# Value products of the last three head pairs: from whole float32 to split 16-bit form

## The chip, the cores and the metric

The kernel runs on one core of a Trainium2 chip. The metric is the device time of one execution in microseconds (us), the median of several runs. TensorE does the matrix products, VectorE and ScalarE work on SBUF and PSUM, GpSimd works on SBUF and issues its own DMAs, and SyncE issues most of the other DMAs.

## The reference

Block-causal attention over 8 batches, 8 heads, 576 positions and 64 columns a head, and behind it a mixture of experts with one expert per token:

```python
scores = scale * np.matmul(q, k.transpose(0, 1, 3, 2))
mask = block_i >= block_j            # blocks of 64 positions
scores = np.where(mask, scores, -1e9)
attn = np.exp(scores - np.max(scores, axis=-1, keepdims=True))
attn = attn / (np.sum(attn, axis=-1, keepdims=True) + 1e-09)
x = np.matmul(attn, v)               # to (4608, 512)
...
e_idx = np.argmax(x @ w_gate, axis=1)
...
h = np.maximum(x[mask] @ w1[e], 0.0) # for each expert e and its tokens
out[mask] = gate_w[mask, None] * eom[mask, e, None] * (h @ w2[e])
```

All inputs and the output are float32.

## The kernel before

Attention works on 32 pairs of heads (pair p is two heads of one batch; four pairs make a batch). The 576 keys of a head are four blocks of 128 (block c is 0 to 3) and an odd block of 64. The work is written out by hand as rounds g = 0 to 135: in each round fixed steps of several pairs are emitted, and each engine executes its instructions strictly in the order of emission. For pair p:

- `prob_tile(3)` in round 4p+4, `prob_tile(0)` and `prob_tile(1)` in 4p+5 and `prob_tile(2)` in 4p+6 compute the scores on TensorE and their exponentials on ScalarE (line 254). Tile 3 holds the odd keys, tile 0 the blocks 1 and 3, tile 1 block 0, tile 2 block 2; the exponentials are float32 in `pcr`, `pc13`, `pc0` and `pc2`.
- `lows(i)` on GpSimd (line 263) makes the low part of a tile: the float32 value less the bfloat16 that is its upper half, stored as float16 (`lpcr` for the odd keys, `lpc` for the others). Tiles 0 and 1 take two instructions, one for each head; tiles 2 and 3 take one.
- `split_v` makes from the loaded values `vn` a float16 high part `vh` (ScalarE, line 155) and a float16 low part `vl` (GpSimd, line 156). It stands in round 4p+7, for the last four pairs in 4p+6.
- `values_odd` multiplies the odd keys' exponentials with the values, and `values(0)` and `values(1)` those of the four blocks for head 0 and head 1: ten products of a 128x128 block with 65 columns per head. They come in rounds 4p+10 and 4p+11, earlier or later for the last pairs: pair 29 in 126 and 127, pair 30 in 129 and 131, pair 31 in 132 and 133. `norm` on VectorE (lines 306 to 310) follows, and then the store and the transposition `turn_x` (line 323).

A block is multiplied in one of two forms. The split form (`splits`, lines 272 to 274) is three 16-bit products: high part with `vh`, high part with `vl`, low part with `vh`. The whole form (line 296) is one float32 product of the exponentials with `vn`; it needs neither `lows` nor `split_v` for that block. `self.whole` lists the blocks that take the whole form: none up to pair 27, block 0 for pair 28, all four for pairs 29, 30 and 31. The odd keys are always split.

Between these steps the rounds carry the start of the expert part. GpSimd scatters the sorted slots of each batch to a table (`tab_d`, line 622), clears the row buffers (line 1072, round 121), reads ids from the table (line 810, round 122) and gathers the first rows (line 821, three gathers at the end of round 124, behind `lows(3)` and ahead of the other `lows` of pair 30). From round 126 on each round casts one quarter of the first expert's weights on ScalarE (line 849) and subtracts on VectorE (line 851: the float32 weights less their high part, both in SBUF), `w1b` first and then `w2b`. SyncE loads the weights (line 885) and the values, and stores the rows. After round 133 come the first expert's products (line 973).

Of the kernel before, what the change touches and what calls it, by code (L numbers as in the profile page):

```python
# [26 lines left out]
def block_attention_top1_moe(  # L27
# [41 lines left out]
    NPR = B * NP  # L69
# [22 lines left out]
    class Pair:  # L92


        def __init__(self, p):
            self.p = p
            self.b, self.hp = divmod(p, NP)
            self.tr = {}
            self.whole = (0, 1, 2, 3) if p >= NPR - 3 else (0,) if p == NPR - 4 else ()

        def fetch(self, queue=None):
            h0 = 2 * self.hp
# [38 lines left out]
        def odd(self, c, ab, c0, c1):  # L141
            return self.tr[c][64 * ab:64 * ab + 64, 0, c0:c1]
# [8 lines left out]
                )  # L151

        def split_v(self):
            sl = slice(2 * len(self.whole), 10)
            nc.scalar.copy(self.vh[:, sl, 0:D], self.vn[:, sl, 0:D])  # L155
            nc.gpsimd.tensor_tensor(self.vl[:, sl], self.vn[:, sl, 0:D], self.vh[:, sl, 0:D], ALU.subtract)  # L156

# [95 lines left out]
                ap = ps[:, :, 0:320]  # L253
            last_exp[0] = nc.scalar.activation(self.pt[i], ap, AF.Exp, scale=SCALE)  # L254

        def lows(self, i):
            if i < 3 and ((1, 3), (0,), (2,))[i][0] in self.whole:
                return
            eng = nc.gpsimd
            n = 2 if i < 2 else 1  # L260
            for ab in range(n):
                sl = slice(ab, ab + 1) if n == 2 else slice(0, 2)
                eng.tensor_tensor(self.pl[i][:, sl], self.pt[i][:, sl], self.high(i)[:, sl], ALU.subtract)  # L263

# [67 lines left out]
    def turn_max(p):  # L332

        z = pairs[p]
        ps = banks()
        pm = ps[:, 0].bitcast(BF16)
        for t in range(NT):
            nc.tensor.transpose(pm[:, P * t:P * t + P], z.nmz[:, t, :], identb)
        z.qe = sb.tile([P, 640], BF16, name="qe")
        nc.scalar.copy(z.qe, pm[:, 0:640])  # L340

    def turn_rest(p, p9):

        ps = banks()
        flat = ps.rearrange("p a n -> p (a n)")
        x = pairs[p].turn_x(flat) if 0 <= p < NPR else iter(())
        y = pairs[p9] if p9 < NPR else None
        next(x, None)
        if y:
            y.turn_blocks(ps[:, 1:2, P:2 * P], 0)  # L350
        next(x, None)
        if y:
            y.halves(ps[:, 1:2, P:2 * P], 0)

    def third(p, between=None):

        ps = banks()
        x, y = (pairs[p] if p < NPR else None), (pairs[p - 1] if p else None)
        if x:
            x.odds([ps[:, ab] for ab in range(2)], 3, 320)  # L360
        if y:
            y.prob_tile(2, ps)
        if between:
            between()
        if x:
            x.max_tile(2)
            last_max[0] = nc.vector.tensor_reduce(x.nm3[:, 1], ps[:, :, 320:384], AX.X, ALU.max, negate=True)
            x.max_rest()
# [70 lines left out]
    def at(g, fn):  # L439
        events.setdefault(max(g, 0), []).append(fn)  # L440

    def opening():


        x, y = Pair(0), Pair(1)
        x.fetch(nc.scalar)
        y.fetch()

        def turned(z, late, ps=None):
            z.turn(owing, ps)  # L450
            one = banks()[:, 0:1, 0:P]
            z.turn_blocks(one, 0)
            z.halves(one, 0, late)

        main = ps_v.tile([P, 2, 512], F32, name="ps_v")
        for i in range(NWARM):
            nc.tensor.matmul(main[:, i % 2], zero16[:, 0:P], zero16, start=True, stop=True)
        turned(x, None, main)
        second.append(lambda: turned(y, owing))
        return x, y  # L460

    with tc.manual_schedule(engines={mybir.EngineType.PE}), tc.high_priority(offset=2000):
        pairs = dict(enumerate(opening()))
# [51 lines left out]
    def pay_later(kind=None):  # L515
        for g in list(later):
            if kind is None or want.get(g) in (None, kind):
                want[g] = next(g, later)
                if want[g] is later:
                    later.remove(g)  # L520
# [529 lines left out]
        at(4 * p - 14, lambda p=p: make(p))  # L1050
    for p in range(NPR):
        at(4 * p + 1, lambda p=p: pairs[p].fetch_v())
        at(4 * p + 6 + (p < NPR - 4), lambda p=p: pairs[p].split_v())
        at(min(4 * p + 13, 4 * NPR + 7), lambda p=p: pairs[p].store())
    at(6, constants)

# [34 lines left out]
    def round_of(g):  # L1091

        r = g % 4

        z = pairs[NPR - 1] if g >= 4 * NPR else None

        def do(back, name, *args):
            p = (g - back) // 4
            if 0 <= p < NPR - (name in LATE):
                getattr(pairs[p], name)(*args)  # L1100

        if r == 0:
            do(4, "prob_tile", 3)
            do(0, "max_tile", 0)
            if g != 4 * NPR:
                do(12, "norm")
            if g == 4 * NPR + 4:
                z.values_odd()
                z.values(0)
            do(4, "lows", 3)  # L1110
        elif r == 1:
            do(5, "prob_tile", 0)
            do(5, "prob_tile", 1)
            do(1, "max_tile", 1)
            do(5, "lows", 0)
            do(5, "lows", 1)
            if g == 4 * NPR + 1:
                pairs[NPR - 2].values_odd()
                pairs[NPR - 2].values(0)
            if g == 4 * NPR + 5:  # L1120
                z.values(1)
                z.norm()
                next(ahead)
                turn_rest(NPR - 2, NPR)
                next(ahead)
        elif r == 2:
            odd = (lambda: do(10, "values_odd")) if g != 4 * NPR + 2 else None
            if g // 4 <= NPR:
                third(g // 4, odd)
            elif odd:  # L1130
                odd()
            while second:
                second.pop(0)()
            while owing:
                owing.pop(0)()
            if g != 4 * NPR + 2:
                do(10, "values", 0)
            if g > 2:
                do(-6, "turn")
            pay_later("m")  # L1140
            pay_later("n")
            pay_later("v")
            do(6, "lows", 2)
        else:
            if g < 4 * NPR:
                turn_max(g // 4)
            if g == 3:
                pairs[2].turn()
            if g < 4 * NPR + 4:
                turn_rest(g // 4 - 3, g // 4 + 2)  # L1150
            else:
                turn_rest(NPR - 1, NPR)
            pay_later("x")
            do(11, "values", 1)
            if g == 4 * NPR - 1:
                pairs[NPR - 3].norm()
        for fn in events.get(g, ()):
            fn()
        pay_later("abwy"[r])
# [4 lines left out]
    with tc.manual_schedule(engines={AT.PE, AT.Activation, AT.DVE, AT.Pool}):  # L1164
        for g in range(NG):
            round_of(g)
            for i in range(FIRST.get(g, 0)):
                next(ahead)
        for what in "papaap":
            if what == "a":  # L1170
                next(ahead)
            else:
                pay_later()
        while later:
            next(ahead, None)
            pay_later()
# [116 lines left out]
```

## Time and profile before

| | before |
|---|---|
| runs | 753.75, 759.34, 760.31 us; median 759.34 |
| profiled execution | 754.9 us, its span 753.3 us |
| TensorE busy | 93% |
| VectorE busy | 68% |
| ScalarE busy | 59% |
| GpSimd busy | 51% |

The span goes from the first to the last instruction of the profiled execution; the rest of its time lies around it. Busy shares are means over the span. In the rows, PE is TensorE (its matrix products), PEld its weight loads, DVE VectorE, ACT ScalarE, POOL GpSimd and SP SyncE; L296 is line 296 of the kernel; `out<-in` names the tiles.

### The profile page before, as it was taken

What the parts mean: (1) busy time and instruction counts of PE and PEld (TensorE: products, weight loads), DVE (VectorE), ACT (ScalarE), POOL (GpSimd) and SP (SyncE); (2) the same over time, 40 slices, a digit from 0 to 9 for tenths busy, and PEclk for the clock granted to TensorE, in tenths of its full rate; (3) what the DMA queues carried; (4) which work ended last, traced back from release to release, by engine and by line L of the source; (5) the groups of instructions that cost most, each with busy time, mean ns of one, the idle gap of its engine ahead of it and who ended that gap; (6) DMA issues with size and microseconds to landing.
All of it is one profiled execution on the core that took longest, in us unless ns stands there. A gap on an engine that the chain in (4) does not pass through costs nothing. (4 is left out here: it accounts for less than half of the span.)

```text
span 753.3 us, 24275 instructions
## 1 busy us (share of the span) xinstructions
PE 699.8 (93%) x9888; PEld 519.6 (69%) x9888; DVE 515.3 (68%) x893; ACT 446.9 (59%) x632; POOL 386.8 (51%) x379
## 2 busy tenths in 40 slices
PE   6899999989988897799899999999999999999994
PEld 4688787867766675678657668676596675776761
DVE  6688686877666767576729789577585785876630
ACT  3676666666555665464129588565685775766530
POOL 1899787869999799533357432222133332210111
PEclk7899999999999999999999999999999999999998
DMA  6655665554587553363085997899999889813501
GB/s 151 150 142 130 147 150 130 134 137 105 120 111 124 109 113 78 66 212 89 18 318 154 320 284 250 262 328 313 299 332 331 243 267 291 170 44 104 185 30 46
DMA packets 207849, 131.60 MB, mean 175 GB/s; under 512 B 161552, under 2 KB 180016, under 8 KB 207728
## 3 DMA queue, kind: packets, MB, share of 16 engines
q1 hardware_dynamic: 198480, 110.36, 55.1%
q0 software_dynamic: 8048, 19.29, 8.1%
q8 instruction: 80, 1.31, 0.8%
q10 hardware_dynamic: 1200, 0.30, 0.2%
q14 instruction: 41, 0.34, 0.2%
HBM read 127.08 MB, written 19.34 MB: 194 GB/s over the span
## 5 line engine op out<-in xcount | busy, mean ns | idle before, releaser
L973 PEld LDWEIGHTS <-w1b 128*128 128x128 f16 (+1 forms) x2208 | 176.4, 98 | 25.1 <-issue 2.7
L973 PE MATMUL ps_s<-xt,w1b 128*128 128x256 f16 (+5 forms) x1920 | 175.5, 253 | 0.6 <-DVE w1b L851 0.3
L1002 PE MATMUL ps_o<-w2b,hh 128*128 128x512 f16 (+1 forms) x560 | 166.6, 379 | 1.1 <-ACT hh L981 0.8
L851 DVE TENSOR_TENSOR w2b<-w2f,w2b 128x1024 bf16<-128x1024 f32 x80 | 92.7, 1220 | 88.4 <-ACT w2b L849 84.3
L263 POOL TENSOR_TENSOR lpc<-pc 128x512 f16<-128x512 f32 x143 | 144.5, 1040 | 7.6 <-ACT pc L254 7.1
L1011 POOL DMA_INDIRECT out_dram<-ys,ids x38 | 45.9, 1208 | 155.3 <-ACT ys L1010 83.9
L1002 PE MATMUL ps_o<-w2b,hl 128*128 128x512 f16 x280 | 106.0, 379 | 0.0
L183 DVE TENSOR_REDUCE nmz<-ps_s 128x2 bf16<-128x896 f32 (+3 forms) x128 | 82.4, 689 | 28.0 <-PE ps_s L169 20.8
L1002 PEld LDWEIGHTS <-hh 128*128 128x128 f16 x560 | 54.3, 98 | 64.3 <-issue 2.0
L254 ACT ACTIVATE pc<-ps_s 128x1024 f32<-128x1024 f32 (+1 forms) x96 | 79.4, 882 | 27.1 <-PE ps_s L218 26.9
L851 DVE TENSOR_TENSOR w1b<-w1f,w1b 128x1024 bf16<-128x1024 f32 x80 | 92.9, 1219 | 1.3 <-ACT w1b L849 1.3
L1010 ACT ACTIVATE ys<-ps_o,ids 128x512 f32<-128x512 f32 (+1 forms) x38 | 26.1, 686 | 107.8 <-PE ps_o L1002 80.2
L131 DVE TENSOR_TENSOR tr<-ps_s,tr 128x128 f16<-128x128 f32 (+1 forms) x63 | 46.9, 750 | 54.7 <-ACT tr L128 48.0
L128 ACT CAST tr<-ps_s 128x128 f16<-128x128 f32 (+1 forms) x63 | 40.6, 648 | 70.5 <-PE ps_s L124 61.4
L849 ACT CAST w1b<-w1f 128x1024 f16<-128x1024 f32 x80 | 78.4, 1045 | 3.4 <-DMA w1f<-in_moe_w_dram 3.0
L849 ACT CAST w2b<-w2f 128x1024 f16<-128x1024 f32 x80 | 77.8, 1043 | 1.1 <-DMA w2f<-in_moe_w_dram 0.9
L821 POOL DMA_INDIRECT xg<-x_d,ids x38 | 50.8, 1337 | 34.8 <-DMA ids<-tab_d 10.0
L274 PE MATMUL ps_v<-vh,lpc 128*128 128x65 f16 x572 | 59.1, 194 | 1.2 <-issue 1.2
L272 PE MATMUL ps_v<-vh,pc 128*128 128x65 f16 x572 | 59.5, 196 | 0.0
L273 PE MATMUL ps_v<-vl,pc 128*128 128x64 f16 x572 | 59.2, 193 | 0.1
L810 POOL DMA_DIRECT2D ids<-tab_d x23 | 16.0, 696 | 83.7 <-DMA out_dram<-ys,ids 71.9
L156 POOL TENSOR_TENSOR vl<-vn,vh 128x640 f16<-128x640 f32 (+2 forms) x32 | 41.8, 1306 | 33.3 <-ACT vh L155 32.9
(226 smaller groups left out, 1470.7 us busy)
## 6 DMA issues: line engine op xcount, KB each, us to landing
w1f<-in_moe_w_dram SPq DMA_DIRECT2D x80, 512.0 KB
w2f<-in_moe_w_dram SPq DMA_DIRECT2D x80, 512.0 KB
nat<-in_k_dram SPq DMA_DIRECT2D x64, 128.0 KB
vn<-in_v_dram SPq DMA_DIRECT2D x64, 128.0 KB
x_d<-xn SPq DMA_DIRECT2D x32, 256.0 KB
nat<-in_q_dram SPq DMA_DIRECT2D x62, 128.0 KB
vn<-in_v_dram SPq DMA_DIRECT2D x64, 32.0 KB
hh<-in_moe_w_dram SPq DMA_DIRECT2D x4, 512.0 KB
```

Source lines behind the costliest of these rows:

```text
L131: nc.vector.tensor_tensor(tl, ps, th, ALU.subtract)
L183: last_max[0] = nc.vector.tensor_reduce(o, ps[:, :, c0:c1], AX.X, ALU.max, negate=True)
L254: last_exp[0] = nc.scalar.activation(self.pt[i], ap, AF.Exp, scale=SCALE)
L263: eng.tensor_tensor(self.pl[i][:, sl], self.pt[i][:, sl], self.high(i)[:, sl], ALU.subtract)
L272: nc.tensor.matmul(o, hi, self.vh[rows, j], start=first, stop=False)
L273: nc.tensor.matmul(o[:, 0:D], hi, self.vl[rows, j], start=False, stop=False)
L274: nc.tensor.matmul(o, lo, self.vh[rows, j], start=False, stop=last)
L821: nc.gpsimd.indirect_dma_start(out=xg[i % NXG][0:width[i], h], out_offset=None, in_=x_d[0:nx, :], in_offset=IOA(ap=ids[i][0:width[i], h, 0 ...
L849: nc.scalar.copy(hi, src)
L851: eng.tensor_tensor(lo[at], src[at], hi[at], ALU.subtract)
L973: nc.tensor.matmul(ph[:, f4].rearrange("p (h n) -> p h n", n=w), wv[:, cc, f, :], xv[:, cc], start=(k == 0), stop=(k == 3 * KD - 1))
L1002: nc.tensor.matmul(py, hv[:, f, h], wv[:, f, :], start=(k == 0), stop=(k == 3 * KF - 1))
```

## The change

Pairs 29, 30 and 31 take the split form: pairs 29 and 30 for all blocks, pair 31 for all but block 2. Pair 28 stays as it was. `split_v` covers all blocks of those three pairs, and that of pair 31 moves from round 130 to round 128. For pair 31 (round 129) the low parts of tiles 0 and 1 are emitted head by head; `lows` skips its tile 2.

```diff
-            self.whole = (0, 1, 2, 3) if p >= NPR - 3 else (0,) if p == NPR - 4 else ()
+            self.whole = (2,) if p == NPR - 1 else (0,) if p == NPR - 4 else ()
...
         def split_v(self):
-            sl = slice(2 * len(self.whole), 10)
+            sl = slice(2 if 0 in self.whole else 0, 10)
...
-        def lows(self, i):
+        def lows(self, i, only=None):
...
-            for ab in range(n):
+            for ab in range(n) if only is None else (only,):
...
-        at(4 * p + 6 + (p < NPR - 4), lambda p=p: pairs[p].split_v())
+        at(4 * p + 6 + (p < NPR - 4) - 2 * (p == NPR - 1), lambda p=p: pairs[p].split_v())
...
-            do(5, "lows", 0)
-            do(5, "lows", 1)
+            if g != 4 * NPR + 1:
+                do(5, "lows", 0)
+                do(5, "lows", 1)
+            else:
+                for ab in range(2):
+                    z.lows(0, ab)
+                    z.lows(1, ab)
```

## Rows read from the trace of the kernel before

**Rows 1.** The page's first part, TensorE to GpSimd: busy us (share) x instructions.

```profile
PE 699.8 (93%) x9888; PEld 519.6 (69%) x9888; DVE 515.3 (68%) x893; ACT 446.9 (59%) x632; POOL 386.8 (51%) x379
```

**Rows 2.** TensorE in order of time: start us, us, engine, line, operation, tiles, count.

```profile
303.87 0.19 PE L272 MATMUL ps_v<-vh,pc 128*128 128x65 f16 x1
...
304.75 0.19 PE L274 MATMUL ps_v<-vh,lpc 128*128 128x65 f16 x1
...
324.61 2.45 PE L296 MATMUL ps_v<-vn,pc 128*128 128x65 f32 x20
...
334.80 0.21 PE L272 MATMUL ps_v<-vh,pcr 64*128 64x65 f16 x2
...
341.88 4.68 PE L296 MATMUL ps_s<-vn,pc 128*128 128x65 f32 x40
```

**Rows 3.** Windows: us, busy PE PEld DVE ACT POOL, PEclk, DMA share, GB/s.

```profile
308.30:341.20 32.90, 30.19 (x478) 24.90 (x477) 22.57 (x62) 18.42 (x31) 13.61 (x15) 0.95 0.66 174
330.60:345.60 15.00, 15.00 (x224) 13.65 (x224) 14.02 (x36) 11.11 (x19) 5.76 (x5) 1.00 0.57 170
320.00:325.00 5.00, 4.95 (x120) 3.49 (x112) 3.73 (x9) 3.13 (x4) 1.94 (x2) 0.93 1.05 349
314.00:317.30 3.30, 1.55 (x20) 1.26 (x17) 2.18 (x5) 0.71 (x2) 0.15 (x1) 1.00 1.05 44
317.30:320.70 3.40, 3.40 (x58) 3.12 (x59) 0.00 (x0) 0.59 (x2) 1.34 (x2) 0.50 0.75 275
```

**Rows 4.** VectorE in order of time; in brackets its idle time and what ended it.

```profile
330.64 1.23 DVE L851 TENSOR_TENSOR w1b<-hh,w1b 128x1024 bf16<-128x1024 f32 x1 [1.89 <-ACT w1b L849]
...
333.19 1.21 DVE L851 TENSOR_TENSOR w1b<-hl,w1b 128x1024 bf16<-128x1024 f32 x1
...
340.83 1.20 DVE L851 TENSOR_TENSOR w2b<-hh,w2b 128x1024 bf16<-128x1024 f32 x1
...
344.40 1.22 DVE L851 TENSOR_TENSOR w2b<-hh,w2b 128x1024 bf16<-128x1024 f32 x1
346.60 0.17 DVE L306 TENSOR_SCALAR sm<-ps_s 128x10 f32<-128x10 f32 x1 [0.98 <-PE ps_s L296]
```

**Rows 5.** GpSimd in order of time, from the clearing of the row buffers on.

```profile
310.66 1.87 POOL L1072 MEMSET xg<- 128x1024 f32 x2
312.69 0.99 POOL L622 DMA_INDIRECT tab_d<-idg,sli  x1 [0.16 <-issue]
...
317.48 0.76 POOL L810 DMA_DIRECT2D ids<-tab_d  x1 [3.33 <-DMA tab_d<-idg,sli]
318.71 0.58 POOL L810 DMA_DIRECT2D ids<-tab_d  x1 [0.46 <-issue]
321.65 1.25 POOL L263 TENSOR_TENSOR lpcr<-pcr 128x640 f16<-128x640 f32 x1 [2.36 <-ACT pcr L254]
324.31 1.06 POOL L821 DMA_INDIRECT xg<-x_d,ids  x1 [1.42 <-DMA ids<-tab_d]
...
333.97 1.54 POOL L263 TENSOR_TENSOR lpcr<-pcr 128x640 f16<-128x640 f32 x1 [3.79 <-ACT pcr L254]
...
341.20 1.73 POOL L622 DMA_INDIRECT tab_d<-idg,sli  x1 [1.31 <-DVE idg L615]
```

**Rows 6.** Groups by line and shape: count, busy us, mean ns, idle before.

```profile
L263 POOL TENSOR_TENSOR lpc<-pc 128x512 f16<-128x512 f32 x143 | 144.5, 1040 | 7.6 <-ACT pc L254 7.1
...
L156 POOL TENSOR_TENSOR vl<-vn,vh 128x640 f16<-128x640 f32 x28 | 39.3, 1404 | 25.0 <-ACT vh L155 24.5 <-issue 0.2
...
L155 ACT CAST vh<-vn 128x640 f16<-128x640 f32 x28 | 21.4, 764 | 0.0
...
L156 POOL TENSOR_TENSOR vl<-vn,vh 128x128 f16<-128x128 f32 x3 | 1.3, 435 | 5.7 <-ACT vh L155 5.7
```

**Rows 7.** GpSimd, then VectorE, in order of time in the expert part.

```profile
421.57 5.76 POOL L821 DMA_INDIRECT xg<-x_d,ids  x1 [6.75 <-DVE xr L935]
...
421.81 4.62 DVE L851 TENSOR_TENSOR w1b<-w1f,w1b 128x1024 bf16<-128x1024 f32 x4
```

## Prediction

> **What bounds the kernel now.** I read the page's first part for the whole [rows 1]: TensorE is busy 93% of 753.3 us, GpSimd 51%. That is an average over an attention part and an expert part, so next I went to the stretch that the change touches, rounds 120 to 133 (about 308 to 350 us), engine by engine in order of time. On TensorE the value products of the last three pairs stand as L296, float32, in one unbroken run after the other [rows 2]; between 330.6 and 345.6 us TensorE has no idle time at all, and VectorE is busy 14.02 of 15.00 us [rows 3], with a queue that runs from the first weight split at 330.64 to the split that ends at 345.62 and then waits only 0.98 us for TensorE before it normalises the last pair at 346.60 [rows 4]. So two engines stand at the end of attention side by side, 1 us apart. GpSimd in the same stretch is busy 13.6 of 32.9 us [rows 3]. It holds scatters, reads of ids and gathers, which wait for DMAs, in a strict order of their own [rows 5].
>
> **What the change takes off TensorE.** A whole block is one float32 product, which the trace shows as two records with two weight loads. The run that starts at 324.61 does 10 blocks (20 records) in 2.45 us: 0.245 us a block; the last 20 blocks take 4.68 us: 0.234 [rows 2]. A split block is three 16-bit products: the second half of pair 28 has 10 split blocks from 303.87 to the start of the 30th product at 304.75, 0.030 us a product, 0.091 a block [rows 2]. I take 0.23 and 0.09, so 0.14 us for each converted block. Pairs 29 and 30 have 20 blocks each; pair 31 converts 16 and keeps the four of key block 2. 56 x 0.14 = 7.8 us of TensorE: 1.4 for each half of pairs 29 and 30, 2.2 for pair 31.
>
> **What it puts on GpSimd.** Low parts: 5 instructions for pair 29, 5 for pair 30, 4 for pair 31 (block 2 is skipped), each 1.04 us [rows 6]: 14.6. The low part of the values now covers ten blocks, 1.40 instead of 0.43 us [rows 6], three times: 2.9. Together 17.5 us, into a stretch with 32.9 - 13.6 = 19.3 us free [rows 3]. The fit leaves 1.8 us for all waits, so order decides. ScalarE's copy for the high part grows to 0.76 us [rows 6], three times; ScalarE is busy 11.1 of the critical 15 us [rows 3], and I cost it at nothing: its own wait before the next exponential covers it, and without that cover it would be at most 0.76 us each. Moving pair 31's value split from round 130 to 128 puts it ahead of the four lows on GpSimd and ahead of two exponentials on ScalarE; it issues no DMA. The values and buffers it needs are free since pair 29's products, so it adds no wait of its own. Interleaving the heads in round 129 lets the products of head 0 start after two lows instead of three; it costs nothing.
>
> **The queue on GpSimd, added up.** Pair 29's four lows come where the clearing of the row buffers started before, at 310.66 [rows 5]: 4.2, so 314.8. Behind them stand the clearing (1.87), a scatter (1.0 and a gap of 0.2), the fifth low (1.04) and the value low (1.40): the scatter ends at 317.9, the queue at 320.3. The first read of ids waits until the scatter has landed; before, it began 3.8 us after the scatter ended [rows 5], so now at 321.7, and the two reads are through at 323.5. Pair 30's odd low (1.25) ends at 324.75. Now the gathers, which stand ahead of pair 30's lows: before, the first began 6.1 us after the first read of ids ended (318.24 to 324.31), with the DMA engines at a share of 1.05 for part of it [rows 3, 5]. That would be 328.5 here; at the other end it can't start before 324.75. I take 326.7, between them, since the transfers that filled the engines at 320 to 325 us are not moved and the reads now come behind them. Three gathers of 1.06 with gaps: 330.5. Five lows: 335.7. The value low of pair 30: 337.1.
>
> To this come waits beside VectorE's weight splits. In the trace GpSimd's odd low at 333.97 took 1.54 us instead of 1.25 when a weight split on VectorE ran over its start (until 334.40), a scatter of 0.99 us took 1.73 over another split [rows 4, 5], and a gather that began at 421.57 took 5.76 us while four splits and one more such operation ran back to back; the splits kept their length [rows 7]. So a split costs the GpSimd instruction beside it between 0.3 and its own 1.2 us. Until 337 two or three splits fall in the queue; I take 2.5 x 0.9 = 2.3, which makes 339.4. Only then can TensorE start pair 30's odd values, which before started at 334.80 [rows 2]: it arrives earlier by up to the 2.8 us saved on pair 29, and stands. After that GpSimd needs 1.25 (odd low of pair 31), 1.40 (its values) and four lows, 4.2: 346.3, plus two splits' 1.8: 348.1. The second half of pair 31 needs the last low; behind it are 8 x 0.09 + 2 x 0.23 = 1.2 us of products: 349.3, where before they ended at 346.56 [rows 2]. The end of attention moves by +2.7, say +3 us: the saved 7.8 is all given back in waiting for lows. The scatters of round 130 and later slip by some 7 us, and I cost that at nothing, because the next work on the table waits for the last batch's logits, far behind; what cover they lose would come back as a late gather.
>
> Here the Trainium skill has a rule, SBUF — State Buffer, section Who interferes with whom: a VectorE instruction with two SBUF inputs and a GpSimd instruction that reads SBUF exclude each other for a whole instruction, and the second to issue blocks fully. The trace agrees for GpSimd (the 1.54 and 5.76 us rows); that VectorE too is held up no row shows. By the rule it would be, which is the third case below.
>
> **How this stands to the runs.** The profiled execution took 754.9 us for a span of 753.3, 1.6 around it. The runs are 753.75, 759.34 and 760.31: the profiled one belongs with the low one, 4.4 under the median. 754.9 + 3 = 757.9; the same on the median is 762.3. The after runs can fall on either side, so I name 760.
>
> **The rivals.**
> Case 1, forecast: GpSimd's queue is late at pairs 30 and 31, +1 to +5 us. For it: the sum above. Against: the gather's start is known to 3.7 us only.
> Case 2, GpSimd keeps up and VectorE's queue becomes the bound. With the gather at 324.75 (-2.0) and no waits beside splits (-4.1) the products end at 343.2. But the queue of VectorE is full from 330.64 to 345.62, and its head can come forward at most by the 1.4 us saved in the half of pair 29 ahead of it: 344.2, against 346.60 before. So -2.4 to +1 us. This also caps any gain: of 7.8 us saved no more than 2.4 can reach the end unless VectorE's queue shrinks, which nothing in the change does.
> Case 3, slower on top of case 1: waits beside splits in both directions, and a lower clock. A weight split that meets a low in progress would wait up to 1.04 us, half on average, seven splits: 3.6 on a queue without idle time. And TensorE, which stands some 5 us before pair 30 and again before pair 31, could fall to the lower clock: after a stretch, 314 to 317.3 us, in which it worked for only 1.55 of 3.30 us, it was granted 0.50, the 1.2 GHz level, from 317.3 to 320.7 [rows 3], which would stretch the last products and first expert work by about 1.5. Together +5 to +9. The point from which it decides: VectorE's last split before the normalisation ends later than the last products.
> Case 4: the full 7.8 us arrive, because the queue of VectorE yields too. Nothing in the rows speaks for it. That the change doesn't do what it says (split blocks slower than 0.09) is excluded by the second half of pair 28, where they stand at it; at most the lower clock doubles it, which is in case 3.
>
> **How the numbers follow.** Case 1: 0.50, case 2: 0.33, case 3: 0.13, case 4: 0.04. The predicted time is case 1's, 760. On either base, case 1 gives 755.9 to 764.3, case 2 752.5 to 760.3, case 3 759.9 to 768.3. 753 to 766 leaves out the top of case 3, case 4 and a corner of case 2. One per cent, about what a measurement of this kernel can tell from no change, is 7.6 us: only case 4 reaches it downwards, 0.05 with the runs' scatter; the top of case 3 upwards, 0.09; 0.86 between. Of the sign I am less sure: about 6 in 10 for slower by anything.
>
> **What would show it.** In the changed profile: runs of L272 to L274 at 0.03 us a product where L296 stood; four or five GpSimd lows after 310 us; the first read of ids near 321.7 and the first gather near 326.7; TensorE idle, waiting for GpSimd's vl, lpc or lpcr, for 3 us or more ahead of pair 30's odd values and again in pair 31; lows of over 1.2 us beside splits. Case 2 shows instead no such wait and VectorE's splits ending last. The prediction is wrong if the gathers start before 325.5 and the lows keep 1.04 us beside splits, or if splits show more than 1.3 us.

## The result, and the profile of the changed kernel

The changed kernel takes 765.29 us (median of 20 runs, 757.47 to 772.89), the kernel before, in 20 runs beside it, 753.72 us: a ratio of 1.0138, 95% interval 1.0116 to 1.0160, so some 10.4 us slower. All ratios and mean clocks here leave out runs over 1.5% above the fastest of their kernel. The profiled execution has a span of 764.5 us at a mean granted clock of 0.976; before it was 753.3 at 0.985.

First the page's first part, which answers to [rows 1]; the page here is the profiler's summary of one execution:

```profile
PE 697.3 (91%) x9922; PEld 515.3 (67%) x9944; DVE 523.6 (68%) x893; ACT 448.9 (59%) x632; POOL 410.1 (54%) x393
```

TensorE is busy for 2.5 us less, in a span that is 11.2 us longer. To see where, I cut out the stretch from the odd low part of pair 29 on GpSimd to the copy of the last batch's gate products out of PSUM (line 549 on ScalarE). Windows of the kernel before, then of the changed kernel; the columns are those of [rows 3]:

```profile
308.27:352.96 44.69, 40.60 (x596) 33.59 (x596) 30.80 (x77) 23.53 (x40) 20.25 (x20) 0.96 0.58 153
```

```profile
305.82:361.78 55.96, 40.04 (x652) 30.56 (x652) 40.12 (x77) 25.21 (x40) 39.74 (x34) 0.82 0.46 123
315.36:325.60 10.24, 5.65 (x68) 5.17 (x68) 5.00 (x6) 1.39 (x3) 3.62 (x4) 0.50 0.92 218
332.42:335.84 3.42, 3.39 (x38) 1.80 (x38) 1.59 (x3) 0.00 (x0) 3.42 (x5) 0.50 0.34 105
346.08:349.49 3.41, 3.41 (x43) 2.87 (x37) 3.41 (x2) 2.77 (x5) 3.41 (x3) 0.50 0.20 62
356.32:359.73 3.41, 3.03 (x15) 2.25 (x14) 3.29 (x7) 2.23 (x4) 2.50 (x3) 0.50 0.61 102
```

The whole loss lies here: 55.96 - 44.69 = 11.27 us. TensorE's busy time is the same within 0.6 us though it has 7.8 us less to do; its clock is 0.82 in place of 0.96. It is idle for 15.92 us where it was idle for 4.09. GpSimd has 19.5 us more. VectorE, whose instructions are the same 77, is "busy" for 9.3 us more. The last four rows are the stretches at the half clock (the 1.2 GHz level): 20.48 us with TensorE working for 15.48, where the kernel before had 3.4 us [rows 3]. At the half clock split products start 0.055 us apart (332.58 to 333.51 us), at the full clock 0.031. If all work there took twice its time, (15.48 - 3.4) / 2 = 6.0 us of busy time would come from the clock; so up to 6.0 us, which is most of why the saved 7.8 don't show.

VectorE's rows say what else happened. VectorE of the changed kernel in order of time, the routing step (lines 655 to 667), which works on tiles of eight columns:

```profile
308.48 0.16 DVE L657 TENSOR_REDUCE f_mx<-cnt 128x1 f32<-128x8 f32 x1
308.68 3.63 DVE L659 SCALAR_TENSOR_TENSOR f_eq<-cnt,f_mx,erev 128x8 f32<-128x8 f32 x1
...
312.53 1.55 DVE L662 TENSOR_SCALAR first<-erev,f_er 128x8 f32<-128x8 f32 x1
...
314.50 3.18 DVE L667 TENSOR_SCALAR row<-t,f_e 128x4 int32<-128x4 f32 x1
317.59 0.82 DVE L183 TENSOR_REDUCE nmz<-ps_s 128x2 bf16<-128x640 f32 x1
```

GpSimd of the changed kernel in the same stretch:

```profile
308.24 4.03 POOL L263 TENSOR_TENSOR lpc<-pc 128x512 f16<-128x512 f32 x4
312.21 1.83 POOL L1072 MEMSET xg<- 128x1024 f32 x2
314.22 1.00 POOL L622 DMA_INDIRECT tab_d<-idg,sli  x1 [0.17 <-issue]
315.24 1.05 POOL L263 TENSOR_TENSOR lpc<-pc 128x512 f16<-128x512 f32 x1
316.24 1.40 POOL L156 TENSOR_TENSOR vl<-vn,vh 128x640 f16<-128x640 f32 x1
```

Line 659, an operation on 128x8, lasts from 308.68 to 312.31: until the four new low parts are through (308.24 + 4.03 = 312.27). Line 667, on 128x4, lasts until the scatter, the fifth low part and the value low are through. The same rows of VectorE of the kernel before:

```profile
311.10 0.23 DVE L659 SCALAR_TENSOR_TENSOR f_eq<-cnt,f_mx,erev 128x8 f32<-128x8 f32 x1
...
311.56 1.00 DVE L662 TENSOR_SCALAR first<-erev,f_er 128x8 f32<-128x8 f32 x1
...
312.98 0.70 DVE L667 TENSOR_SCALAR row<-t,f_e 128x4 int32<-128x4 f32 x1
313.41 1.28 DVE L183 TENSOR_REDUCE nmz<-ps_s 128x2 bf16<-128x640 f32 x2
```

There line 659 took 0.23 us. Lines 662 and 667 stood even then: they end at 312.56 and 313.68, with the memset (310.66 + 1.87 = 312.53) and the scatter (312.69 + 0.99 = 313.68) of [rows 5]; elsewhere in the runs below either takes 0.23. From line 657 to the maxima behind them (line 183) VectorE needs 9.1 us; in the kernel before it was 2.5, from 310.91 on. So a maximum that TensorE waits for comes 6.6 us late. TensorE of the changed kernel, in order of time, where it meets that:

```profile
318.93 0.50 PE L338 MATMUL ps_s<-identb,nmz 128*128 128x128 bf16 x3 [7.17 <-DVE nmz L183]
```

The weight splits, which the prediction let keep their 1.2 us [rows 4], stretch too. VectorE of the changed kernel, line 851, and then GpSimd beside it:

```profile
338.15 1.59 DVE L851 TENSOR_TENSOR w1b<-hh,w1b 128x1024 bf16<-128x1024 f32 x1 [3.86 <-ACT w1b L849]
340.97 2.30 DVE L851 TENSOR_TENSOR w1b<-hl,w1b 128x1024 bf16<-128x1024 f32 x1
345.70 1.91 DVE L851 TENSOR_TENSOR w1b<-hh,w1b 128x1024 bf16<-128x1024 f32 x1
347.54 2.05 DVE L851 TENSOR_TENSOR w1b<-hl,w1b 128x1024 bf16<-128x1024 f32 x1
```

```profile
342.15 2.38 POOL L156 TENSOR_TENSOR vl<-vn,vh 128x640 f16<-128x640 f32 x1
344.50 5.99 POOL L263 TENSOR_TENSOR lpc<-pc 128x512 f16<-128x512 f32 x4
```

Here the two take turns: each side loses one instruction of the other's at a time (four splits 7.85 us in place of 4.9, the value low 2.38 in place of 1.40, four lows 5.99 in place of 4.0). TensorE never waits for GpSimd in this execution, which was the forecast's mechanism.

### The profile page after: what moved, and what is told of

Read it like the earlier page. It is cut to its first block, busy times and chain, and to the rows that moved or that the text cites. A ratio compares the mean times of both kernels' runs of the same rounds, so it can differ in the third digit from the quotient of the medians.

```text
span 764.5 us, 24383 instructions
## 1 busy us (share of the span) xinstructions
PE 697.3 (91%) x9922; PEld 515.3 (67%) x9944; DVE 523.6 (68%) x893; ACT 448.9 (59%) x632; POOL 410.1 (54%) x393
## 5 line engine op out<-in xcount | busy, mean ns | idle before, releaser
L263 POOL TENSOR_TENSOR lpc<-pc 128x512 f16<-128x512 f32 x157 | 160.7, 1055 | 8.1 <-ACT pc L254 7.5
L1002 PE MATMUL ps_o<-w2b,hh 128*128 128x512 f16 (+1 forms) x538 | 162.0, 379 | 1.2 <-ACT hh L981 0.8
L1011 POOL DMA_INDIRECT out_dram<-ys,ids x38 | 48.7, 1282 | 154.4 <-ACT ys L1010 82.8
L272 PE MATMUL ps_v<-vh,pc 128*128 128x65 f16 x612 | 64.8, 197 | 0.8 <-issue 0.8
L273 PE MATMUL ps_v<-vl,pc 128*128 128x64 f16 x612 | 64.6, 195 | 0.6 <-issue 0.5
L274 PE MATMUL ps_v<-vh,lpc 128*128 128x65 f16 x612 | 64.3, 195 | 0.0
L272 PEld LDWEIGHTS <-pc 128*128 128x128 bf16 x628 | 59.1, 100 | 7.4 <-issue 7.3
```

The costliest lines, as they stand in the source:

```text
L272: nc.tensor.matmul(o, hi, self.vh[rows, j], start=first, stop=False)
L273: nc.tensor.matmul(o[:, 0:D], hi, self.vl[rows, j], start=False, stop=False)
L274: nc.tensor.matmul(o, lo, self.vh[rows, j], start=False, stop=last)
L1002: nc.tensor.matmul(py, hv[:, f, h], wv[:, f, :], start=(k == 0), stop=(k == 3 * KF - 1))
L1011: nc.gpsimd.indirect_dma_start(out=out, out_offset=IOA(ap=ids[i][0:w, h, 0:1].bitcast(U32), axis=0), in_=ys[0:w], in_offset=None, bounds_c ...
```

## The experiments

Each kernel was timed beside the kernel before on the same chip. The mean granted clock is given with each, since part of the loss lies there: for the kernel before it was 0.9849 beside the first four runs and 0.9885 beside the others.

**Pair 29 alone.** Of the kernel before, `self.whole` starts one pair later:

```
-self.whole = (0, 1, 2, 3) if p >= NPR - 3 else ...
+self.whole = (0, 1, 2, 3) if p >= NPR - 2 else ...
```

> Pair 29 alone goes over to split products; pairs 30 and 31 keep their whole ones. Theory A (the loss starts where pair 29's low parts, written by GpSimd, stand beside the routing steps of VectorE, lines 655 to 667): the loss is here almost in full, less the 2.8 us that 20 blocks save, so 5 to 9 us slower than the kernel before, with line 659 above 3 us and TensorE's wait at line 338 above 4 us. Theory B (what pairs 30 and 31 add, late low parts or lengthened weight splits, makes the loss): 3 us faster to 1 us slower.

1.0139 (1.0096 to 1.0183), clock 0.9718: all of the loss with 20 of the 56 blocks. VectorE of this kernel, in order of time:

```profile
316.76 3.65 DVE L659 SCALAR_TENSOR_TENSOR f_eq<-cnt,f_mx,erev 128x8 f32<-128x8 f32 x1
...
322.61 3.18 DVE L667 TENSOR_SCALAR row<-t,f_e 128x4 int32<-128x4 f32 x1
```

The same standstill, to 0.02 us, and the same wait of TensorE at line 338, 7.2 us. That is what theory A said. The next run spoiled it.

**Pairs 30 and 31, not 29.** Of the changed kernel; `split_v` leaves out the whole blocks of pair 29 as well:

```
-self.whole = (2,) if p == NPR - 1 else ...
+self.whole = (2,) if p == NPR - 1 else (0, 1, 2, 3) if p == NPR - 3 else ...
```

> Pairs 30 and 31 as in the changed kernel, pair 29 whole as before. Theory A: line 659 is back at some 0.2 us and TensorE's wait at line 338 under 2 us; the products of 36 blocks save 5.0 us, the lengthened weight splits cost up to 3 us, so 3 us faster to 2 us slower than before. Theory B: 6 to 10 us slower, with the wait at line 338 as before.

1.0157 (1.0123 to 1.0192), clock 0.9735: the whole loss again, some 11.8 us, without pair 29. Line 659 is back at 0.23 us and TensorE's long wait at line 338 is gone, as theory A has it, but the time isn't what it expected. So two causes would each make all of it, or one cause sits in both places. Of this kernel, VectorE in order of time, GpSimd in order of time, and the waits of TensorE (total, times, longest):

```profile
325.87 12.75 DVE L851 TENSOR_TENSOR w1b<-hh,w1b 128x1024 bf16<-128x1024 f32 x1 [4.88 <-ACT w1b L849]
```

```profile
324.59 5.03 POOL L263 TENSOR_TENSOR lpc<-pc 128x512 f16<-128x512 f32 x5
329.59 1.39 POOL L156 TENSOR_TENSOR vl<-vn,vh 128x640 f16<-128x640 f32 x1
330.95 1.24 POOL L263 TENSOR_TENSOR lpcr<-pcr 128x640 f16<-128x640 f32 x1
332.16 1.39 POOL L156 TENSOR_TENSOR vl<-vn,vh 128x640 f16<-128x640 f32 x1
333.52 4.02 POOL L263 TENSOR_TENSOR lpc<-pc 128x512 f16<-128x512 f32 x4
```

```profile
PE ps_v L272 <- DVE xn L310: 10.3, 1, 10.3
```

One weight split of 1.2 us stands from 325.87 to 338.62, until GpSimd's unbroken run of twelve subtractions has ended at 337.54, and then does its work. Pair 30's normalisation (line 306) is queued behind it, TensorE waits for the bank that it frees, and from within that wait on the clock is at half for 17.1 us (332.1 to 349.1). So theory A had the mechanism, but took one of its places for all of it.

**The routing step one round earlier,** in the changed kernel and, as a control, in the kernel before:

```
+at(4 * NPR - 9, route_first)
 at(4 * NPR - 8, start_first)     # and no longer called in load_first
```

> The changed kernel with the whole routing step (lines 655 to 667) one round earlier, ahead of the round whose low parts it ran into; the loads that it feeds stay where they are. Theory A: each of its operations is back under 1.2 us, TensorE's wait at line 338 is under 2 us, and 6 to 10 us of the 10 come back (2 us faster to 4 us slower than before). Theory B: 8 to 12 us slower than before, since nothing of pairs 30 and 31 is changed.

> The kernel before with the same move of the routing step one round earlier. It shows what the move gives without the change: both theories 2 us faster to 1 us slower than before, since lines 662 to 667 waited there for a memset and a scatter of GpSimd, some 1 to 2 us. The difference between this run and the run of the changed kernel with the move is what the change is worth without the collision: by theory A 3 us faster to 3 us slower.

The control is even: 1.0002 (0.9965 to 1.0038), clock 0.9865. The changed kernel comes to 1.0086 (1.0050 to 1.0121), clock 0.9740: some 3.9 us come back, of the 6 to 10 that theory A expected; by the medians of all runs, 1.0141 against 1.0154, hardly any. The routing step is back under 0.6 us an operation, and the standstill has moved on. VectorE and then the waits of TensorE:

```profile
335.26 12.74 DVE L851 TENSOR_TENSOR w1b<-hh,w1b 128x1024 bf16<-128x1024 f32 x1
```

```profile
PE ps_v L273 <- POOL vl L156: 9.5, 2, 8.5
```

This is the forecast's own wait: in this execution the low parts of pair 30 came late (the gathers ahead of them ran to 333.9 us), and the late run then held VectorE as well.

**A wider theory.** Theory D: VectorE's operation stands wherever it meets a run of GpSimd's subtractions; the clock falls in TensorE's wait. Theory E: split products are dearer in themselves. Four runs; pair 29 with the routing step out of its way, both kernels with GpSimd's queue in another order, and breaks in GpSimd's run:

> Pair 29 alone in split products, with the routing step one round earlier. Theory A was too narrow: in the runs so far a subtraction of VectorE that takes two operands from SBUF stands still while GpSimd works off a run of subtractions (line 659 for 3.6 us in one run, the weight split at line 851 for 12.75 and 12.74 us in two others), and TensorE's clock falls in the wait that follows. Theory D (this standstill, wherever the two meet): with the routing step out of the way nothing long of VectorE meets the low parts of pair 29, so 3 us faster to 2 us slower than before, and no operation of VectorE above 3 us between 300 and 350 us. Theory E (the split products themselves cost more than they save, by the clock): 6 to 10 us slower, as the run of pair 29 alone.

> The changed kernel with the routing step one round earlier and GpSimd's queue put in another order: the reads of the ids and the gathers stand behind the low parts of pairs 30 and 31 and not ahead of them, so that the low parts come in short runs, each when its exponentials are ready, and not in one run of 12 us. Theory D: no weight split above 4 us, TensorE's wait ahead of pair 31's products under 3 us, and 4 us faster to 4 us slower than before; what may eat it up is a gather that comes too late for line 909. Theory E: 8 to 12 us slower, as the changed kernel.

> The kernel before with the same two moves, as the control of the run with both moves: the low parts are not there, so both theories expect 2 us faster to 2 us slower than before.

> Pairs 30 and 31 split, pair 29 whole, with a memset of eight columns on GpSimd behind each of its subtractions for these two pairs. It asks whether VectorE's subtraction gets in where GpSimd's run has a break. If it does: no weight split above 3.5 us, and 3 to 9 us faster than the run without the breaks. If the run holds VectorE through the breaks too: the weight split again at 10 us or more and no gain.

The new order takes the two reads of ids and the three gathers out of their place ahead of pair 30's low parts:

```
-fetch_ids(steps[0]); fetch_ids(steps[1], (0, 1))        # ahead of the first split
-fetch_x(steps[0]); fetch_x(steps[1], (0, 1))
 for w, fn in ((w1, split_w1), (w2, split_w2)):
     for c in range(4):
         yield "wyab"[c]
+        if (w is w2, c) == (False, 1): ...fetch_ids...
+        if (w is w2, c) == (True, 0): ...fetch_x...
```

Pair 29 without the collision: 1.0061 (1.0010 to 1.0111), clock 0.9842; without the move it was 1.0139. But only four of its ten runs are in this ratio; the medians of all runs, 757.60 and 746.04 us, are 1.0155 apart. So this run doesn't tell how much of pair 29's loss goes with the collision. In its profiled execution (758.08 us, not one of the four) no operation of VectorE is above 1.85 us between 300 and 350 us, as theory D expected, and yet the clock is at half for 30.7 us, between 307 and 314 and between 331 and 355 us. What took it down there is open.

With both moves the changed kernel has 1.0068 (1.0031 to 1.0106), clock 0.9791, and the control 1.0012 (0.9969 to 1.0055), clock 0.9872. Of the changed kernel with both moves, VectorE, GpSimd and the waits of TensorE:

```profile
326.31 2.58 DVE L851 TENSOR_TENSOR w1b<-hh,w1b 128x1024 bf16<-128x1024 f32 x1 [2.43 <-ACT w1b L849]
...
335.75 2.06 DVE L851 TENSOR_TENSOR w1b<-hl,w1b 128x1024 bf16<-128x1024 f32 x1
```

```profile
321.41 5.03 POOL L263 TENSOR_TENSOR lpc<-pc 128x512 f16<-128x512 f32 x5
326.41 1.40 POOL L156 TENSOR_TENSOR vl<-vn,vh 128x640 f16<-128x640 f32 x1
...
332.71 6.00 POOL L263 TENSOR_TENSOR lpc<-pc 128x512 f16<-128x512 f32 x4
338.86 1.07 POOL L821 DMA_INDIRECT xg<-x_d,ids  x1 [0.15 <-issue]
```

```profile
PE ps_s L921 <- DMA xg<-x_d,ids: 2.3, 1, 2.3
```

The long standstill is gone, and half of the loss with it; the 5.1 us that are left are above the 4 that theory D allowed for. It did not go for the reason that the expectation gave: GpSimd's run is not short, nine subtractions without a break from 317.84 to 327.81 us, but the split now comes 1.5 us before its end. Two things are left: the gather now comes late, as the expectation feared, and the clock is at half for 10.2 us between 334 and 351, for 3.4 ahead of the wait for the gather and for 6.8 behind it.

The breaks of eight columns did nothing for the standstill: 1.0101 (1.0060 to 1.0142), clock 0.9820, from four runs, where the kernel without them had 1.0157 (1.0123 to 1.0192). VectorE, then GpSimd:

```profile
323.53 12.96 DVE L858 TENSOR_TENSOR w1b<-hh,w1b 128x1024 bf16<-128x1024 f32 x1
```

```profile
322.97 0.12 POOL L93 MEMSET gap<- 128x8 f32 x1
323.04 1.05 POOL L268 TENSOR_TENSOR lpc<-pc 128x512 f16<-128x512 f32 x1
```

The memset fills the place between two subtractions without leaving any: each instruction begins before the one ahead has ended.

**Less for GpSimd, and products that keep TensorE busy.**

> Pairs 29 and 30 in split products, pair 31 whole, with the routing step one round earlier and the ids' reads and the gathers behind the low parts of pair 30. GpSimd has 7 us less to do for pair 31, TensorE 2.2 us more. Theory D with the clock (a standstill or a late gather makes TensorE wait, and each such wait takes the clock down to half for 3.4 to 17 us): no weight split above 3 us, no wait of TensorE above 2.5 us between 305 and 350 us, a clock like that of the control with the two moves, and 5 to 0 us faster than before. Theory E (split products are dearer in themselves): 3 to 7 us slower than before, 40 of 56 parts of the loss.

> The changed kernel with 42 products of zeros put into TensorE's queue where its profile shows TensorE waiting: 24 of 512 columns ahead of the transposes at line 338 of pair 30 (5.2 us of a wait of 7.2), 6 of 448 ahead of line 599, 6 of 512 ahead of each of the first two groups of transposes at line 920. They write PSUM that is overwritten afterwards; nothing waits less. If the lower clock after a wait is a large part of the loss: the mean clock rises from 0.975 towards 0.982 and 3 to 6 us of the loss come back. If the waits alone are the loss: no change, or 1 to 3 us more.

> The changed kernel with both moves (routing step earlier, gathers behind the low parts), and 18 products of zeros where its profile showed TensorE waiting: 6 ahead of line 599, 8 and 4 ahead of the first two groups of transposes. If the clock is what is left of its loss: the mean clock rises from 0.979 to that of the control, 0.986, and it comes out 1 to 5 us faster than before. If the late gather itself is what is left: as without the products, 3 to 6 us slower.

```
+for i in range(24):      # line 338, pair 30 (and 6 each at lines 599 and 920)
+    nc.tensor.matmul(ps[:, 1], zero16[:, 0:P], zero16, start=True, stop=True)
```

Two pairs, with both moves, pair 31 whole: 0.9997 (0.9965 to 1.0028), clock 0.9852. Its longest weight split is 2.57 us and TensorE's longest wait 2.4, as theory D expected. Theory E falls here: 40 of the 56 blocks are split, and nothing is lost. But nothing is gained either, at the lower end of what theory D expected. Time multiplied by the mean clock, which is what the run would take at the full clock, if TensorE worked throughout the stretches at half, is 734.3 us (mean of 10 runs) against 737.1 for the kernel before (22 runs): 2.8 us less. Time at half clock is 22.1 us a run against 17.1, worth up to 2.5. So what is saved at the full clock is about what the clock takes back; by which way isn't shown.

The products of zeros in the changed kernel, in its own order, made it worse: 1.0254 (1.0220 to 1.0289), clock 0.9777. VectorE:

```profile
305.02 6.05 DVE L673 TENSOR_SCALAR row<-t,f_e 128x4 int32<-128x4 f32 x1
...
330.68 11.71 DVE L857 TENSOR_TENSOR w1b<-hh,w1b 128x1024 bf16<-128x1024 f32 x1 [2.65 <-ACT w1b L855]
```

In this execution the standstill struck in both places, and the products of zeros came after the clock had fallen at 310.1 us, so most of them ran at half of it. This run says nothing for or against the clock's part. In the kernel with both moves the clock did what was expected, 0.9856, with 21.5 us a run at half in place of 31.4. The time came out between the two expectations: 1.0024 (0.9995 to 1.0053) where it had 1.0068 without them, so some 1.8 us slower than before and not 1 to 5 faster. The two intervals overlap slightly, so the 3.3 us between them are likely, not certain.

**The disputed cost by itself.**

> The disputed cost by itself; nothing of the reference is computed, and its time means nothing. GpSimd works off six subtractions like the low parts (128x512, some 1.0 us each), and VectorE asks for one operation at a time that is set by small memsets, in steps, to a point of that run: 24 trials with a subtraction like the weight split (128x1024, two operands in SBUF, 1.2 us alone), then three points each for the same with one operand in PSUM, a copy with one operand, a 128x4 operation with one and with two operands in SBUF, a maximum over 1024 columns, and three weight splits in a row. The runs so far, sorted by when the weight split came after the start of the GpSimd instruction then running: up to 0.21 us it got in behind that one instruction (1.9 us), from 0.28 us on it stood until the whole run was over. Theory D with that rule: in the 24 trials it gets in early for points in the first 0.2 to 0.28 us of an instruction of GpSimd and stands until the run's end, up to 5 us, for the others; the operation with an operand in PSUM and the maximum take their time alone. Rival (it depends on something else, such as what VectorE did just before or where the data lies): all 24 alike, all standing or all in turns.

```
for i in range(ticks): nc.vector.memset(tick, 0.0)
op()                                                    # VectorE
for i in range(6): nc.gpsimd.tensor_tensor(go, ga, high, ALU.subtract)
```

VectorE, then GpSimd, one row of a kind (line 88: two operands in SBUF; 91: one in PSUM; 94: a copy of one operand in SBUF; 97: 128x4, one operand in SBUF; 103: maximum; the last row two of three splits in a row):

```profile
15.56 2.10 DVE L88 TENSOR_TENSOR do<-da,db 128x1024 bf16<-128x1024 f32 x1
...
207.44 1.21 DVE L91 TENSOR_TENSOR do<-pa,db 128x1024 bf16<-128x1024 f32 x1
...
221.79 1.14 DVE L94 CAST do<-da 128x1024 bf16<-128x1024 f32 x1
...
244.51 0.61 DVE L97 TENSOR_SCALAR so<-sm 128x4 f32<-128x4 f32 x1
...
288.78 1.21 DVE L103 TENSOR_REDUCE ended<-da 128x1 f32<-128x1024 f32 x1
...
311.69 3.92 DVE L88 TENSOR_TENSOR do<-da,db 128x1024 bf16<-128x1024 f32 x2
```

```profile
15.53 7.48 POOL L113 TENSOR_TENSOR go<-ga 128x512 f16<-128x512 f32 x6
...
206.42 6.63 POOL L113 TENSOR_TENSOR go<-ga 128x512 f16<-128x512 f32 x6
```

With an operand in PSUM, or as a maximum, VectorE takes its time alone (1.21 us) and GpSimd's six take 6.62 or 6.63 us in all six trials. With both operands in SBUF VectorE's operation waits for the instruction in flight, 2.10 us at most, and GpSimd loses 0.85 us or a little more. One operand in SBUF is enough to be held: the copy, 0.68 us alone, took 1.14 and 0.84 in two of its three trials, and the operation on 128x4, 0.16 us alone, 0.61 and 0.32; the 128x4 operation with two operands took the same. So "both operands in SBUF", which the expectations had, is too narrow. And the rule that I had drawn from the kernels is wrong: in all 24 trials, whatever the point, VectorE got in behind the one instruction. A difference is in the rows: six subtractions take 6.63 us here, 1.10 each, of which 1.04 is the subtraction and the rest a gap (all write one tile, so each probably waits for the end of the last); in the kernels five take 5.03, 1.01 each. Between these there is no gap. That a gap lets VectorE in fits this run and the standstills; the turns taken in the changed kernel, in the four lows from 344.50 on, where there is no gap either, it doesn't explain. A kernel whose low parts wait for one another was not tried.

## Why the prediction was wrong in its mechanism, step by step

The sign was right and the time inside the range, but the forecast's case was not what happened, and that the time lies inside is luck. The forecast was 3 us on top of the kernel before, and the most that a case had was 9; some 10.4 us came. The upper end of the range, 766, rests on the median of three runs, 759.34, and 20 runs gave 753.72. More than one per cent slower had a chance of 0.09.

- What comes off TensorE: right. The thirty split products of the first half of pair 30 start between 342.34 and 343.24 us, 0.031 us from one to the next, as taken from [rows 2].
- GpSimd's added work: 17.5 us forecast, 19.5 measured. In it are 2.9 us of turns with the weight splits, 0.98 for the value low and 1.96 for the four lows; 0.3 to 1.2 us a split were forecast, about 1.0 each were found.
- GpSimd's dates: ids 321.7 forecast, 322.0 measured (319.58 with 2.45 us added for the shift of this trace's axis: the odd low of pair 29 starts at 305.82, and at 308.27 before); first gather 326.7 against 330.5, since the odd low of pair 30 ahead of it waited for a late ScalarE; value low of pair 30 done at 339.4 against 341.1. That the last date fits to 1.7 us is luck in part: the gather was 3.8 us late, and the 2.3 us for waits beside splits did not come, since the first split now starts at 338.15. The queue didn't set the end, because TensorE was later still.
- The step that failed: "the splits kept their length". From one row, in which GpSimd's gather stood and VectorE's splits did not [rows 7], I took the harm to go one way ("that VectorE too is held up no row shows"; lines 662 and 667 of the kernel before, 1.00 and 0.70 us, show it), and priced the other way only in case 3, at half a low, 0.5 us for each split. The runs showed 3.6 and 3.2 us for two tiny operations, which I had not looked for at all, since the low parts of pair 29 were costed against GpSimd's own queue alone, and up to 12.75 us for a split. The Trainium skill, SBUF — State Buffer, section Who interferes with whom, has the rule that was set aside: whoever issues first has the shared pair, and the other blocks fully. The runs agree, and go beyond it: it speaks of a whole instruction, and here VectorE stood through eleven.
- Case 3 named the lower clock at +1.5 us; it cost up to 6.0 in the profiled execution and up to 6.6 over the runs ((36.0 - 22.8) / 2, mean us at half clock of 17 runs and of 23 of the kernel before). Its direction was right and its chance of 0.13 too low. Its point was met as well: pair 31's last product starts at 352.52 us, and VectorE's last split before the normalisation ends at 356.00, so the normalisation begins at 355.92 without a wait. But the greater part of the loss came earlier, at lines 659 to 667 (maxima 6.6 us late), which the case didn't have.
- "TensorE idle, waiting for GpSimd": not in the changed kernel's profile, but 8.5 us in the run with the routing step moved. The forecast's wait is real, and stands behind the other.
- "The prediction is wrong if ... splits show more than 1.3 us": they did, 1.59 to 2.30 us.

In sum: VectorE's standstill beside GpSimd's low parts is shown, in six kernels, at three lines (659, 667, 851). That moving the two apart takes half of the loss away is shown with all 56 blocks; all of it went only where pair 31 was left whole too, so the other half isn't split between the late gather, pair 31's low parts and the clock. The clock's part is bounded (up to 6.6 of some 10 us) and supported by the products of zeros, not separated cleanly. Why VectorE gets its turn in some runs of GpSimd's and stands through others is open.

## What to carry to other kernels

When work is moved to an idle engine, list what runs beside it on the other engines, down to operations of eight columns: an operation's length in the old trace holds only beside the old neighbours. Put long runs of GpSimd's subtractions where VectorE reads PSUM or reduces, and not beside its subtractions, copies or small operations on tiles in SBUF. Work taken off TensorE is a gain only where TensorE doesn't then wait; a wait of a few us can also cost the clock, here in stretches of 3.4 to 17 us, so look at the granted clock of the stretch before counting the saving.

## What the runs showed of the hardware that was not expected

- A VectorE instruction with two operands in SBUF stood for 12.75, 12.74, 12.96 and 11.71 us in four kernels, until a run of GpSimd's subtractions ended; memsets of 0.1 us inside the run (12.96) did not let it in.
- Where both queues are full and VectorE has got in once, they take turns, one instruction each: 1.9 to 2.1 us for a split of 1.2, and 5.99 for four lows that take 4.03 alone.
- An operand in PSUM, or a reduction, is free of this on both sides: 1.21 us, and 6.63 for GpSimd's six. One operand in SBUF is not: 1.14 us for a copy of 0.68.
- The kernel before spends 17 to 23 us of a run at the half clock level on average; its fastest profiled relative, the control with both moves, had none between 5 and 732 us and a span of 739.8.
